# Gated attention and MLP mix on one core: five buffers of exponentials instead of six, a reordered start of attention, late products every second cycle, and one weight load behind shifted copies

## The chip, the cores and the metric

The kernel runs on one core of one Trainium2 chip. The core has five engines that work side by side and wait for each other through semaphores: TensorE (PE in the profile; its weight loads are PEld), VectorE (DVE), ScalarE (ACT), GpSimd (POOL) and SyncE (SP), which here issues most of the transfers. The metric is device time in microseconds (us). The kernel before takes 921.9 us as the median of 3 runs (921.63 to 922.75).

## The reference

The input x has 2048 tokens of 448 features. Two branches work on it, and a gate per token mixes them (cut to what matters):

```python
x = A_x                                             # (1, 2048, 448)
g = sigmoid((x * gate_w).sum(-1, keepdims=True))
# A: attention, 16 heads of 28 features, one key and one value head for all
q = (x @ wq) in 16 heads;  k = x @ wk;  v = x @ wv
p = softmax(q k^T * 28 ** -0.5);  a = concat(p v) @ wo
# B: shifts along the tokens, then an MLP
h  = gelu(layernorm(x) @ w1)
hs = concat(four quarters of h, shifted by +1, -1, +2, -2 tokens) @ w2
x1 = x + hs
b  = x1 + gelu(layernorm(x1) @ w3) @ w4
out = g * a + (1 - g) * b
```

## The kernel before

Everything is in one program without loops on the chip; the Python loops unroll. Each engine runs its instructions in the order in which the Python code issues them (`manual_schedule` over all five engines), and a semaphore wait is put ahead of an instruction whose data or whose buffer is not yet free. So the order in the code sets the order of work on every queue, SP's included.

Matrices are split into a high and a low part (`wh`, `wl`, `ah`, `al`), and a product is three matrix products that accumulate in one bank of PSUM.

**Stage 1** (to about 126 us) makes the queries, keys and values, the product with w1 (`stage_w1`) and the product with w2 (`stage_w2`). For the shifts, `spare_h(b)` copies rows of `hl` into the spare partitions of `hh` and `hl` with four transfers (L433 to L436); the last block's products with w2 read those spare partitions. At the end of stage 1 three things are issued on SP, in this order: `load_w34(0, s2a)`, which loads the first 256 columns of w3 (L611) and the first 256 rows of w4 (L612) into `w34raw`; `xt_read(0, ...)`, which loads the normalised x1 of the first block in transposed form into `xr` (L177 and twice L179); and `spare_h(NB - 1)`.

**Stage 2** (126 to about 401 us) is the MLP with w3 and w4, four blocks of 512 tokens. A piece of it is left for later: the products of the last 128 rows of w4 for the last block (`w4_late`, `gf_late`) are cut into 8 jobs, two halves of the columns for each of 4 tiles of tokens. A job is 16 matrix products (L843) and one add into `x1` by DVE (L878). That add needs rows of `x1` which POOL has multiplied with 1 - g (`weigh_x1`, L670).

**Stage 3** (about 401 to 908 us) is attention. A unit u is one block of 512 queries and a group of 4 heads; there are 16 units, and each goes over 16 key tiles of 128 keys. The loop runs over cycles c of two key tiles each, 128 in all; c = 8u + i. PSUM has 8 banks: four singles (`bank_0` to `bank_3`) and two pairs (`pair_0`, `pair_1`). In a cycle TensorE does, in this order:

- the scores of the first tile (L205, for 4 heads): heads 0 and 1 into two singles, heads 2 and 3 into `pairs[0]`;
- the scores of the second tile: into the other two singles and `pairs[1]`;
- the values of the two tiles of the cycle before (L892): exponentials `p` times `vext`, one half of the queries into the first single of this cycle (`s0`), the other half into the second (`s1`), each once ScalarE has read the scores there;
- one job, if there is one (L843), into the free half of `s0`.

ScalarE makes the exponentials (L258) in this order: first tile, heads 0 and 1, one by one; second tile, heads 0 and 1, one by one; second tile, heads 2 and 3 at once from `pairs[1]`; first tile, heads 2 and 3 at once. These last two heads DVE has copied from `pairs[0]` into the tile `p` before (L939), so that the pair is free early, and ScalarE works there in place. DVE also adds the values to the output (L813, L817). The exponentials of a key tile are one tile `p`; its pool has `PB = 6` buffers, used in turn. The first key tile's `p_0_0` is in another pool.

In cycle 0 the first tile's scores are already there: they were made in stage 2, between the products with w4, in the four singles. So cycle 0 makes the scores of the second tile, in `bank_2`, `bank_3` and `pair_1`, and then two w4 jobs, in `bank_0` and `bank_1`. Cycles 1 to 6 do one w4 job each; cycles 7 to 11 have no job. From cycle 12 on (unit 1, i = 4) there are jobs of the product with wo, 8 for each unit, and each cycle does one.

Of the kernel before, what the change touches and what calls it, by code (L numbers as in the profile page):

```python
# [29 lines left out]
SCALE = DH ** -0.5  # L30
EPS = 1e-5
SHIFTS = (-1, 1, -2, 2)
PB = 6
MK = 16
LIMIT = 1e18

# [1 line left out]
def f32(ap):  # L38
    return ap.bitcast(F32)
# [3 lines left out]
def gated_mix_kernel(  # L43
# [12 lines left out]
    nc = tc.nc  # L56
# [14 lines left out]
    first = keep.tile([P, 4], F32, name="first")  # L71
# [103 lines left out]
    def xt_read(b, raw):  # L175
        xd = xd_of.pop(b)
        nc.sync.dma_start(raw[:, 0:3, :], xd[0:12].rearrange("(c f) i p u -> (f i) c (p u)", c=3))  # L177
        for k in (0, 64):
            nc.sync.dma_start(raw[k:k + 64, 3, :], xd[12:14].rearrange("f i p u -> (f i) (p u)"))  # L179
# [16 lines left out]
    def q_low(u):  # L196
        nc.vector.tensor_sub(ql_of[u], qr_of.pop(u), f32(qh_of[u]))

    def scores(u, kt, ps):
        kh = kh_of[0]  # L200
        keys = slice(kt * P, (kt + 1) * P)
        for r, (k, q) in enumerate(((kh, qh_of[u]), (kh, ql_of[u]), (kl, qh_of[u]))):
            for j in range(4):
                h = slice(32 * j, 32 * j + 32)
                nc.tensor.matmul(ps[j], k[h, keys], q[h, :], start=(r == 0), stop=(r == 2), tile_position=(32 * j, 0))  # L205
# [51 lines left out]
    def exps(p, heads, source=None):  # L257
        nc.scalar.activation(p[:, heads], p[:, heads] if source is None else source, AF.Exp, scale=SCALE)  # L258
# [4 lines left out]
    with tc.tile_pool(name="s1b", bufs=1) as s1b, \  # L263
            tc.tile_pool(name="ps1", bufs=1, space=PSUM) as ps1:
        s1_stack = ExitStack()
        s1 = s1_stack.enter_context(tc.tile_pool(name="s1", bufs=1))
# [154 lines left out]
        def shifted(t, m, k):  # L421

            c = [1 + SHIFTS[i] - SHIFTS[0] + 516 * i for i in range(m, m + k)]
            flat = f32(t)[C:P].rearrange("i m n -> i (m n)")
            if k == 1:
                return flat[:, c[0]:c[0] + 512]
            step = c[1] - c[0]
            o = min(c[0], 4 * 516 - 2 * step)
            return flat[:, o:o + 2 * step].rearrange("i (m n) -> i m n", m=2)[:, :, c[0] - o:c[0] - o + 512]

        def spare_h(b):
            low = f32(hl[b])
            nc.sync.dma_start(shifted(hh[b], 0, 2), low[0:32, 0, 1:513])  # L433
            nc.sync.dma_start(shifted(hh[b], 2, 2), low[32:64, 0, 1:513])
            nc.sync.dma_start(shifted(hl[b], 1, 2), low[64:96, 0, 1:513])
            nc.sync.dma_start(shifted(hl[b], 3, 1), low[96:112, 0, 1:513])  # L436
# [158 lines left out]
        s2a = ctx2.enter_context(tc.tile_pool(name="s2a", bufs=1, side="right", reuse_waits="tile"))  # L595
# [4 lines left out]
        def big(name):  # L600
            return bigs.tile([P, 2048], F32, tag="big", bufs=2, name=name)

        def load_w34(i, pool):
            w3h.append(pool.tile([P, 4, 2 * P], F32R, name=f"w3h_{i}"))
            w3l.append(pool.tile([P, 4, 2 * P], F32R, name=f"w3l_{i}"))
            w4h.append(pool.tile([P, 2, D], F32R, name=f"w4h_{i}"))
            w4l.append(pool.tile([P, 2, D], F32R, name=f"w4l_{i}"))
            raw = big(f"w34raw_{i}")
            raw3[i] = raw[:, 0:1024].rearrange("p (c n) -> p c n", c=4)
            raw4[i] = raw[:, 1024:1024 + 2 * D].rearrange("p (c n) -> p c n", c=2)  # L610
            nc.sync.dma_start(raw3[i], w3[:, :, i * 256:i * 256 + 256])  # L611
            nc.sync.dma_start(raw4[i], w4[i * 256:i * 256 + 256, :].rearrange("(c p) n -> p c n", p=P))  # L612
# [27 lines left out]
                    nc.vector.tensor_sub(hi[64:128], raw[64:128], f32(hi)[64:128])  # L640

        xraw2[0] = big("xr_0").rearrange("p (c n) -> p c n", c=4)
        load_w34(0, s2a)
        xt_read(0, xraw2[0])
        spare_h(NB - 1)

        def third(t):
            if t == 0:
# [17 lines left out]
    with tc.tile_pool(name="s2", bufs=1, reuse_waits="tile") as s2, \  # L666
# [35 lines left out]
        for b in range(NB):  # L702
            acc = [ps2.tile([P, 512], F32, tag="acc", bufs=4, name=f"acc_{b}_{t}") for t in range(4)]
            gs = {}
            for f in range(NF):
# [26 lines left out]
                if b == 1 and f == 1:  # L732
                    nc.gpsimd.memset(khd, 0.0)
                    for j in range(4):
                        h = slice(32 * j, 32 * j + DH)
# [33 lines left out]
    with tc.tile_pool(name="s3", bufs=1, reuse_waits="tile") as s3, \  # L769
# [4 lines left out]
        pairs = [ps3.tile([P, 2, 512], F32, name=f"pair_{i}") for i in range(2)]  # L774
# [105 lines left out]

        p_of = {0: p_first}

        def score_tiles(u, kt, first, second, pair):
            scores(u, kt, [first, second, pair[:, 0], pair[:, 1]])
            p_of[u * NT + kt] = p = s3.tile([P, 4, 512], F32, tag="p", bufs=PB, name=f"p_{u}_{kt}")
            return p

# [7 lines left out]
                    p_of.pop(k)  # L895

        jobs = [(w4_products, w4_add, (t,), cols) for t in range(4) for cols in halves]
        left, right, both = slice(0, 1), slice(1, 2), slice(2, 4)
        sums, norms, later = [], [], []
        pv = None  # L900
        MAX_AT = 2
# [1 line left out]
        def job_products(ps, n):  # L903
            adds = []
            for _ in range(min(n, len(jobs))):
                products, add, args, cols = jobs.pop(0)
                part = ps[:, 0:D // 2] if n == 1 else ps[:, cols]
                products(*args, part, cols)
                adds.append((add, args, part, cols))
            return adds  # L910
# [5 lines left out]
        def run_jobs(ps, n):  # L916
            job_adds(job_products(ps, n))

        NC = NU * NT // 2
        HINTS = {8 * NT // 2 + 4: [mybir.EngineType.SP],  # L920
                 14 * NT // 2 - 2: [mybir.EngineType.DVE, mybir.EngineType.Activation]}
        for c in range(NC):
            u, i = divmod(c, NT // 2)
            k = 2 * c
            s0, s1, s2, s3_ = singles if c % 2 == 0 else singles[2:] + singles[:2]
            if c:
                pa = score_tiles(u, 2 * i, s0, s1, pairs[0])
                with tc.block() if c in HINTS else nullcontext():
                    if c in HINTS:
                        tc.mark_branch_hint_location("redo", "LikelyTaken", HINTS[c])  # L930
                    exps(pa, left, s0.unsqueeze(1))
                exps(pa, right, s1.unsqueeze(1))
            if i == 2 and u == 0:
                q_begin(1)
            if i == 3 and u == 0:
                q_low(1)
                q_fetch(2)
            if 0 < c < NC - 1:
                nc.vector.tensor_copy(pa[:, both], pairs[0])  # L939
            elif c:  # L940
                exps(pa, both, pairs[0])
            if i == 3 and later:
                later.pop(0)()
            if i == 1 and sums:
                norms.append(recip(*sums.pop()))
            if i == (3 if u == NU - 1 else 4) and norms:
                w = norms[0][0]
                norm(*norms.pop())
            if i == 5 and u + 2 < NU:
                q_begin(u + 2)  # L950
            if i == 6 and u + 2 < NU:
                q_low(u + 2)
                q_fetch(u + 3)
            pb = score_tiles(u, 2 * i + 1, s2, s3_, pairs[1])
            exps(pb, left, s2.unsqueeze(1))
            exps(pb, right, s3_.unsqueeze(1))
            exps(pb, both, pairs[1])
            if 0 < c < NC - 1:
                exps(pa, both)
            if u and i == (3 if u == NU - 1 else 4):  # L960
                jobs += [(wo_products, wo_add, (u - 1, t), cols) for t in range(4) for cols in halves]
            if c == 0:
                run_jobs(s0, 1)
                run_jobs(s1, 1)
                continue
            v = (c - 1) // (NT // 2)
            at_max = i == MAX_AT and u + 1 < NU
            q0, q1 = slice(0, 256), slice(256, 512)
            values((k - 2, k - 1), s0[:, q0], q0)
            values_end(v, s0[:, q0], q0)  # L970
            if at_max:
                max_part(u + 1, range(4), pairs[0][:, 0])
                later.append(lambda u=u: max_end(u + 1))
            elif i == MAX_AT:
                run_jobs(pairs[0][:, 0], 1)
            values((k - 2, k - 1), s1[:, q0], q1)
            adds = job_products(s0[:, q1], 1)
            values_end(v, s1[:, q0], q1)
            job_adds(adds)
            if i == 0 and v < NU - 1:  # L980
                sums.append(sums_begin(v))
        assert not sums and not norms and not later and len(jobs) == 3

        u = NU - 1
# [7 lines left out]

        for k in (2 * NC - 2, 2 * NC - 1):
            for i in range(2):
# [60 lines left out]
        with tc.If(again > 0, label="redo"):  # L1055
            for b in range(NB):
                for g in range(NG):
                    u = b * NG + g
# [6 lines left out]
                    for kt in range(NT):  # L1065
                        ps = [bank(f"s2_{u}_{kt}_{j}") for j in range(4)]
                        scores(u, kt, ps)
                        p = s3.tile([P, 4, 512], F32, tag="p", bufs=PB, name=f"p2_{u}_{kt}")
                        for j in range(4):
# [7 lines left out]
                    for t in range(4):  # L1077
                        ps = bank(f"wo2_{u}_{t}")[:, whole]
# [55 lines left out]
```

## Time and profile before

| what | time |
|---|---|
| median of 3 runs | 921.9 us |
| lowest and highest of them | 921.63 and 922.75 us |
| the profiled execution | 921.32 us |
| its span, from the first to the last instruction | 919.5 us |
| granted clock of TensorE | 1.00 in all of it |

1.8 us of the profiled execution lie outside the span. Times in the rows that follow are from the start of the span. A row of the timeline gives the start, the length, the engine, the line, the operation, output and inputs, the shapes, how many instructions the row merges, and in brackets the idle time ahead of it with what ended it. Buffer numbers are left out of the names there: `bank` is any of the four singles, `pair` any of the two pairs, `p` any tile of exponentials. The ends of matrix products are modelled, and they overlap in the array, so that a row's length is more than the time from one product to the next.

### The profile page before, as it was taken

Reading aid. Unit: us, or ns where it says so; the run is one execution under the profiler, and the core shown is the slowest. Engines: PE = TensorE matmul, PEld = TensorE weight load, DVE = VectorE, ACT = ScalarE, POOL = GpSimd, SP = SyncE. Lnnn points to the kernel's source line nnn. Section 1 sums busy time; section 2 is a strip of 40 time slices with the busy share of each in tenths; the row PEclk is TensorE's granted clock in tenths of the full one; section 3 lists DMA queues with packets and bytes.
Section 4 is the critical chain, followed back from the end, with each engine's and each line's share of the span. In section 5 each row is a group of like instructions: output and inputs, shape, how many; then the busy total and the mean of one; then the engine's idle time right before and its main releaser. Section 6 shows DMA issues by size and latency. Waiting matters only on the chain.

```text
span 919.5 us, 24276 instructions
## 1 busy us (share of the span) xinstructions
PE 907.3 (99%) x10360; PEld 626.2 (68%) x10360; DVE 516.7 (56%) x961; ACT 636.9 (69%) x1003; POOL 78.6 (9%) x116
## 2 busy tenths in 40 slices
PE   9999999999999999999999999999999999999998
PEld 6788888888888888865555555555555555555554
DVE  3674274631441431146676776777667767767665
ACT  5442255322222222269999999999999999999995
POOL 3153420200000520020000000000000000000000
PEclk9999999999999999999999999999999999999999
DMA  9832643120110110010000001000011000010001
GB/s 300 274 102 66 174 134 127 40 66 1 41 47 1 40 46 1 1 52 24 17 23 23 15 22 48 24 25 15 25 33 37 24 18 20 15 54 14 15 14 43
DMA packets 40583, 47.32 MB, mean 51 GB/s; under 512 B 10136, under 2 KB 28632, under 8 KB 40472
## 3 DMA queue, kind: packets, MB, share of 16 engines
q1 hardware_dynamic: 37304, 40.30, 15.2%
q10 hardware_dynamic: 3168, 5.44, 1.6%
q8 instruction: 82, 1.34, 0.6%
q14 instruction: 29, 0.24, 0.1%
HBM read 32.56 MB, written 11.67 MB: 48 GB/s over the span
## 4 chain that ended last, share of the span: by engine, by line
PE 92%; ACT 4%; DMA 1%; issue 1%; DVE 0%; SPq 0%; POOL 0%; ACTq 0%
PE bank L892 26%; PE bank L205 17%; PE bank L843 5%; PE acc L700 5%; PE acc L698 5%; PE acc L699 5%; PE g L136 4%; PE g L137 4%; PE g L138 4%; ACT p L258 4%; PE pair L205 1%; PE g L139 1%; PE g L140 1%; PE h L137 1%; PE h L136 1%; PE h L138 1%
## 5 line engine op out<-in xcount | busy, mean ns | idle before, releaser
L258 ACT ACTIVATE p<-bank 128x512 f32<-128x512 f32 x514 | 267.0, 610 | 9.0 <-PE bank L205 2.0
L892 PE MATMUL bank<-p,vext 128*32 128x256 f32 x4064 | 247.7, 382 | 5.5 <-ACT p L258 1.0
L892 PEld LDWEIGHTS bank<-p,vext 128*32 128x32 f32 x4064 | 117.6, 109 | 123.2 <-ACT p L258 60.0
L939 DVE COPY p<-pair 128x1024 f32<-128x1024 f32 x126 | 154.3, 1225 | 57.2 <-PE pair L205 43.3
L688 ACT ACTIVATE gh<-g 128x512 fp32r<-128x512 f32 x55 | 33.0, 599 | 182.6 <-PE g L140 182.6
L817 DVE TENSOR_TENSOR o<-o,bank 128x256 f32<-128x256 f32 x222 | 93.5, 421 | 86.0 <-PE bank L892 72.2
L258 ACT ACTIVATE p<-p 128x1024 f32<-128x1024 f32 x126 | 138.8, 1102 | 0.0
L258 ACT ACTIVATE p<-pair 128x1024 f32<-128x1024 f32 x129 | 137.4, 1065 | 0.0
L690 DVE TENSOR_TENSOR gl<-gf,gh 128x512 fp32r<-128x512 f32 x55 | 38.3, 697 | 166.4 <-ACT gf L689 166.4
L205 PE MATMUL bank<-qh,kh 32*128 32x512 f32 x514 | 115.5, 443 | 0.3 <-DVE x L878 0.2
L205 PE MATMUL pair<-qh,kh 32*128 32x512 f32 x510 | 114.3, 443 | 0.0
L205 PE MATMUL bank<-qh,kl 32*128 32x512 f32 x514 | 102.1, 389 | 0.0
L205 PE MATMUL bank<-ql,kh 32*128 32x512 f32 x514 | 102.0, 389 | 0.0
L205 PE MATMUL pair<-qh,kl 32*128 32x512 f32 x510 | 101.1, 389 | 0.0
L205 PE MATMUL pair<-ql,kh 32*128 32x512 f32 x510 | 100.8, 389 | 0.0
L205 PEld LDWEIGHTS bank<-qh,kh 32*128 32x128 f32 x514 | 48.1, 181 | 62.8 <-issue 38.0
L700 PE MATMUL acc<-w4h,gl 128*128 128x448 f32 x220 | 80.7, 367 | 0.0
L698 PE MATMUL acc<-w4h,gh 128*128 128x448 f32 x220 | 80.1, 364 | 0.0
L699 PE MATMUL acc<-w4l,gh 128*128 128x448 f32 x220 | 79.8, 363 | 0.0
L843 PE MATMUL bank<-wof,on 128*32 128x224 f32 (+1 forms) x984 | 69.5, 357 | 0.1
L137 PE MATMUL g<-al,w3h 128*128 128x512 f32 x168 | 65.4, 389 | 0.0
L136 PE MATMUL g<-ah,w3h 128*128 128x512 f32 x168 | 65.4, 389 | 0.0
(206 smaller groups left out, 1393.0 us busy)
## 6 DMA issues: line engine op xcount, KB each, us to landing
qd<-qf ACTq DMA_DIRECT2D x15, 256.0 KB
rb<-rd SPq DMA_DIRECT2D x15, 256.0 KB
x<-in_x_dram SPq DMA_DIRECT2D x4, 896.0 KB
xd<-xt SPq DMA_DIRECT2D x16, 224.0 KB
w34raw<-in_w_dram SPq DMA_DIRECT2D x7, 512.0 KB
qr<-qd SPq DMA_DIRECT2D x64, 56.0 KB
w34raw<-in_w_dram SPq DMA_DIRECT2D x7, 448.0 KB
out_dram<-ot SPq DMA_DIRECT2D x14, 224.0 KB
```

The source lines that it names most:

```text
L136: nc.tensor.matmul(ps, wh[:, c, :], ah[:, c, :], start=(c == 0), stop=False)
L137: nc.tensor.matmul(ps, wh[:, c, :], al[:, c, :], start=False, stop=False)
L138: nc.tensor.matmul(ps, wl[:, c, :], ah[:, c, :], start=False, stop=False)
L205: nc.tensor.matmul(ps[j], k[h, keys], q[h, :], start=(r == 0), stop=(r == 2), tile_position=(32 * j, 0))
L258: nc.scalar.activation(p[:, heads], p[:, heads] if source is None else source, AF.Exp, scale=SCALE)
L698: nc.tensor.matmul(ps, gh[:, tok], w4h[i][:, k, :], start=(f == 0), stop=False)
L699: nc.tensor.matmul(ps, gh[:, tok], w4l[i][:, k, :], start=False, stop=False)
L700: nc.tensor.matmul(ps, gl[:, tok], w4h[i][:, k, :], start=False, stop=(f == stop))
L817: nc.vector.tensor_add(o, o, pv)
L843: nc.tensor.matmul(ps[32 * i:32 * i + 32, :], a[:, c:c + 32], w, start=start, stop=stop, tile_position=(0, 32 * i))
L892: nc.tensor.matmul(pv[32 * j:32 * j + 32, :], vext[:, kt, :], p_of[k][:, j, qs], start=(k == ks[0]), stop=(k == ks[-1]), tile_position=(0, ...
L939: nc.vector.tensor_copy(pa[:, both], pairs[0])
```

## The change

Four edits, in the words of the code:

- `PB` goes from 6 to 5.
- `load_w34(0, s2a)` moves behind `spare_h(NB - 1)`, so that on SP the two loads of w3 and w4 come behind the transfers of `xr` and the four copies of `spare_h`.
- In cycle 0 the second tile's scores go into the four singles alone, and the third tile's scores, which were cycle 1's first ones, follow at once, in the two pairs. DVE copies heads 0 and 1 of the third tile out of `pair_0`, and ScalarE takes heads 2 and 3 from `pair_1` and then the copy. Cycle 0 now does three w4 jobs, two in `bank_2` and one in `bank_3`. The two pairs then change their parts for the rest (`pairs.reverse()`), and cycle 1 has only its second tile left.
- The other five w4 jobs are in cycles 3, 5, 7, 9 and 11, one each, instead of cycles 1 to 6.

```diff
-PB = 6
+PB = 5
...
         xraw2[0] = big("xr_0").rearrange("p (c n) -> p c n", c=4)
-        load_w34(0, s2a)
         xt_read(0, xraw2[0])
         spare_h(NB - 1)
+        load_w34(0, s2a)
...
-        def score_tiles(u, kt, first, second, pair):
-            scores(u, kt, [first, second, pair[:, 0], pair[:, 1]])
+        def score_tiles(u, kt, first, second, third, fourth):
+            scores(u, kt, [first, second, third, fourth])
             p_of[u * NT + kt] = p = s3.tile([P, 4, 512], F32, tag="p", bufs=PB, name=f"p_{u}_{kt}")
             return p
...
-        left, right, both = slice(0, 1), slice(1, 2), slice(2, 4)
+        left, right, both, front = slice(0, 1), slice(1, 2), slice(2, 4), slice(0, 2)
...
         NC = NU * NT // 2
+        JOBS_0 = (2, 1)
+        IDLE = range(2, 12, 2)
...
         for c in range(NC):
             u, i = divmod(c, NT // 2)
             k = 2 * c
             s0, s1, s2, s3_ = singles if c % 2 == 0 else singles[2:] + singles[:2]
-            if c:
-                pa = score_tiles(u, 2 * i, s0, s1, pairs[0])
+            if c == 0:
+                pb = score_tiles(u, 1, s2, s3_, s0, s1)
+                for j, ps in enumerate((s2, s3_, s0, s1)):
+                    exps(pb, slice(j, j + 1), ps.unsqueeze(1))
+                pa = score_tiles(u, 2, *(q[:, h] for q in pairs for h in range(2)))
+                nc.vector.tensor_copy(pa[:, front], pairs[0])
+                for ps, n in zip((s2, s3_), JOBS_0):
+                    run_jobs(ps, n)
+                exps(pa, both, pairs[1])
+                exps(pa, front)
+                pairs.reverse()
+                continue
+            if c > 1:
+                pa = score_tiles(u, 2 * i, s0, s1, pairs[0][:, 0], pairs[0][:, 1])
...
-            if 0 < c < NC - 1:
+            if 1 < c < NC - 1:
                 nc.vector.tensor_copy(pa[:, both], pairs[0])
-            elif c:
+            elif c > 1:
                 exps(pa, both, pairs[0])
...
-            pb = score_tiles(u, 2 * i + 1, s2, s3_, pairs[1])
+            pb = score_tiles(u, 2 * i + 1, s2, s3_, pairs[1][:, 0], pairs[1][:, 1])
             exps(pb, left, s2.unsqueeze(1))
             exps(pb, right, s3_.unsqueeze(1))
             exps(pb, both, pairs[1])
-            if 0 < c < NC - 1:
+            if 1 < c < NC - 1:
                 exps(pa, both)
...
-            if c == 0:
-                run_jobs(s0, 1)
-                run_jobs(s1, 1)
-                continue
...
-            adds = job_products(s0[:, q1], 1)
+            adds = job_products(s0[:, q1], 0 if c in IDLE or c == 1 else 1)
```

What this does to the order on the engines is shown at three places. In these rows a bracket names the semaphores that an instruction waits for.

The first place is ScalarE in two cycles of unit 5, as they stand in every cycle of attention but the first few: the tiles 8 to 11, where `p_5_8` and `p_5_10` are first tiles of their cycles. Before:

```order
L258 ACTIVATE p_5_8_6007<-bank_0_3209 128x512 [waits PE_49,Activation_49]
L258 ACTIVATE p_5_8_6007<-bank_1_3210 128x512 [waits PE_49]
L258 ACTIVATE p_5_9_6025<-bank_2_3211 128x512 [waits DVE_49,PE_49]
L258 ACTIVATE p_5_9_6025<-bank_3_3212 128x512 [waits PE_49]
L258 ACTIVATE p_5_9_6025<-pair_1_3259 128x1024 [waits PE_49]
L258 ACTIVATE p_5_8_6007<-p_5_8_6007 128x1024 [waits DVE_49]
L258 ACTIVATE p_5_10_6066<-bank_2_3211 128x512 [waits PE_49,Activation_49]
```

And in the changed kernel:

```order
L258 ACTIVATE p_5_8_6007<-bank_0_3209 128x512 [waits PE_49]
L258 ACTIVATE p_5_8_6007<-bank_1_3210 128x512 [waits PE_49]
L258 ACTIVATE p_5_9_6025<-bank_2_3211 128x512 [waits DVE_49,PE_49,Activation_49]
L258 ACTIVATE p_5_9_6025<-bank_3_3212 128x512 [waits PE_49]
L258 ACTIVATE p_5_9_6025<-pair_0_3258 128x1024 [waits PE_49]
L258 ACTIVATE p_5_8_6007<-p_5_8_6007 128x1024 [waits DVE_49]
L258 ACTIVATE p_5_10_6066<-bank_2_3211 128x512 [waits PE_49]
```

The instructions and their order are the same. With six buffers a cycle's first tile always gets a buffer that an earlier first tile had, whose last write was ScalarE's own, in place, and so the first exponentials of a cycle wait for ScalarE's semaphore beside TensorE's. With five buffers, first and second tiles change buffers in turn, and that second wait moves to the first exponentials of the second tile.

The second place is SP at the end of stage 1. Before:

```order
L611 DMA w34raw_1064<-in_w_dram 128x4x256 [waits DMAHW5_49,PE_49]
L612 DMA w34raw_1064<-in_w_dram 128x2x448 [waits DMAHW6_49]
L177 DMA xr_1059<-xd_892 128x3x512 [waits DMAHW7_49]
L179 DMA xr_1059<-xd_892 64x512 [waits DMAHW0_49]
L179 DMA xr_1059<-xd_892 64x512 [waits DMAHW1_49]
L433 DMA hh_957<-hl_958 16x2x512 [waits DMAHW2_49,Pool_49]
L434 DMA hh_957<-hl_958 16x2x512 [waits DMAHW3_49]
L435 DMA hl_958<-hl_958 16x2x512 [waits DMAHW4_49]
L436 DMA hl_958<-hl_958 16x512 [waits DMAHW5_49]
```

And in the changed kernel:

```order
L177 DMA xr_1059<-xd_892 128x3x512 [waits DMAHW5_49,PE_49]
L179 DMA xr_1059<-xd_892 64x512 [waits DMAHW6_49]
L179 DMA xr_1059<-xd_892 64x512 [waits DMAHW7_49]
L433 DMA hh_957<-hl_958 16x2x512 [waits DMAHW0_49,Pool_49]
L434 DMA hh_957<-hl_958 16x2x512 [waits DMAHW1_49]
L435 DMA hl_958<-hl_958 16x2x512 [waits DMAHW2_49]
L436 DMA hl_958<-hl_958 16x512 [waits DMAHW3_49]
L611 DMA w34raw_1071<-in_w_dram 128x4x256 [waits DMAHW4_49]
L612 DMA w34raw_1071<-in_w_dram 128x2x448 [waits DMAHW5_49]
```

The two weight loads go to the end. The wait for TensorE (a buffer of stage 1 that becomes free) stays with whichever transfer is first. The semaphores named DMAHW are eight that transfers use in turn, so that the load of w4 now waits for the first transfer of `xr`, which has the same one (5).

The third place is TensorE at the start of attention, from the last scores of the second key tile to the first values. Before:

```order
L205 MATMUL pair_1_3259<-qh0_1049,kl_77 128x512 x2
L843 MATMUL bank_0_3209<-w4_late_1052,gf_late_1051 32x224 x4
L843 MATMUL bank_1_3210<-w4_late_1052,gf_late_1051 32x224 x4
L205 MATMUL bank_2_3211<-qh0_1049,kh_1048 128x512 [waits Activation_49]
L205 MATMUL bank_3_3212<-qh0_1049,kh_1048 128x512 [waits Activation_49]
L205 MATMUL pair_0_3258<-qh0_1049,kh_1048 128x512 [waits DVE_49]
...
L205 MATMUL bank_0_3209<-qh0_1049,kh_1048 128x512 [waits DVE_49]
L205 MATMUL bank_1_3210<-qh0_1049,kh_1048 128x512 [waits DVE_49]
L205 MATMUL pair_1_3259<-qh0_1049,kh_1048 128x512 [waits Activation_49]
...
L892 MATMUL bank_2_3211<-p_0_0_3226,vext_78 32x256 [waits Activation_49]
```

And in the changed kernel:

```order
L205 MATMUL bank_1_3210<-qh0_1049,kl_77 128x512
L205 MATMUL pair_0_3258<-qh0_1049,kh_1048 128x512 [waits DVE_49]
...
L843 MATMUL bank_2_3211<-w4_late_1052,gf_late_1051 32x224 [waits Activation_49]
L843 MATMUL bank_2_3211<-w4_late_1052,gf_late_1051 32x224 x7
L843 MATMUL bank_3_3212<-w4_late_1052,gf_late_1051 32x224 [waits Activation_49]
L843 MATMUL bank_3_3212<-w4_late_1052,gf_late_1051 32x224 x3
L205 MATMUL bank_0_3209<-qh0_1049,kh_1048 128x512 [waits Activation_49]
L205 MATMUL bank_1_3210<-qh0_1049,kh_1048 128x512 [waits Activation_49]
L205 MATMUL pair_0_3258<-qh0_1049,kh_1048 128x512 [waits DVE_49]
...
L892 MATMUL bank_2_3211<-p_0_0_3226,vext_78 32x256 [waits DVE_49]
```

The third tile's scores stand ahead of the jobs, in the pairs. The fourth tile's scores wait for exponentials and for DVE's copy, no longer for the adds of the jobs (L878); that wait moves to the first values.

## The prediction

> **What bounds the kernel now.** I read the page first: the busy times and the chain of work that ended last.
>
> ```profile
> PE 907.3 (99%) x10360; PEld 626.2 (68%) x10360; DVE 516.7 (56%) x961; ACT 636.9 (69%) x1003; POOL 78.6 (9%) x116
> PE 92%; ACT 4%; DMA 1%; issue 1%; DVE 0%; SPq 0%; POOL 0%; ACTq 0%
> ```
>
> TensorE looks full, but 4% of the chain is ScalarE's, so somewhere TensorE waits for ScalarE, again and again. The chain by time and the timeline, in one cycle of attention (c = 20, and the start of 21), show where:
>
> ```profile
> 479.30 0.61 ACT p L258
> 479.91 0.04 issue
> 479.95 1.93 PE bank L892 x32
> ```
>
> ```profile
> 478.82 0.39 PE L205 MATMUL pair<-qh,kl 32*128 32x512 f32 x2
> 479.30 2.07 ACT L258 ACTIVATE p<-bank 128x512 f32<-128x512 f32 x4
> 479.50 0.39 PE L205 MATMUL bank<-qh,kl 32*128 32x512 f32 x2
> 479.52 0.39 PE L205 MATMUL pair<-qh,kl 32*128 32x512 f32 x2
> 479.95 1.93 PE L892 MATMUL bank<-p,vext 128*32 128x256 f32 x32
> 481.23 1.06 ACT L258 ACTIVATE p<-pair 128x1024 f32<-128x1024 f32 x1
> 481.70 0.56 PE L843 MATMUL bank<-wof,on 128*32 128x224 f32 x8
> 482.13 1.10 ACT L258 ACTIVATE p<-p 128x1024 f32<-128x1024 f32 x1
> 482.77 0.40 PE L205 MATMUL pair<-qh,kl 32*128 32x512 f32 x2
> 483.26 1.09 ACT L258 ACTIVATE p<-bank 128x512 f32<-128x512 f32 x2
> ```
>
> This is a closed loop over two engines: scores of the first tile end (478.82 + 0.39 = 479.21), ScalarE's first exponentials (0.61 from 479.30), values into the bank that they read (479.95), the job (481.70), the next scores (ready at 483.17), exponentials again at 483.26. The period is 3.96 here. A gap in this loop is paid once per cycle. One gap is between the scores' end and ScalarE's start: 0.09, at both places.
>
> **Part 1: five buffers.** The order shows that with six the loop's exponentials wait for TensorE and for ScalarE itself, with five for TensorE alone. The same instruction with one wait stands in cycles 2 and 3, where buffers are used for the first time; a long idle time ahead of it is there too, so I put beside it cycle 19, where ScalarE was idle as well and which has both waits.
>
> ```profile
> 408.13 0.39 PE L205 MATMUL pair<-qh,kl 32*128 32x512 f32 x2
> 408.55 2.07 ACT L258 ACTIVATE p<-bank 128x512 f32<-128x512 f32 x4 [0.41 <-PE pair L205]
> 412.27 0.39 PE L205 MATMUL pair<-qh,kl 32*128 32x512 f32 x2
> 412.69 2.07 ACT L258 ACTIVATE p<-bank 128x512 f32<-128x512 f32 x4 [0.21 <-PE pair L205]
> ...
> 474.11 1.10 ACT L258 ACTIVATE p<-p 128x1024 f32<-128x1024 f32 x1
> 474.87 0.39 PE L205 MATMUL pair<-qh,kl 32*128 32x512 f32 x1
> 475.35 1.09 ACT L258 ACTIVATE p<-bank 128x512 f32<-128x512 f32 x2
> ```
>
> One wait: 408.52 to 408.55 and 412.66 to 412.69, 0.03. Two waits: 475.26 to 475.35, 0.09, although ScalarE had been idle since 475.21. So the second wait costs about 0.06, not ScalarE's own pace. The Trainium skill ("Perfetto Trace Analysis", Identifying Dependency Chains) says that an instruction that waits on several engines may get an extra semaphore instruction put ahead of it; it has no price for one, and the trace's 0.09 against 0.03 agrees with it.
>
> Does the loop keep the 0.06? TensorE must be able to start the values earlier. Its last scores start at 479.52, the values at 479.95, 0.43 later; in cycle 2 the same two starts were, by the timeline, 0.36 apart, and without a wait for ScalarE the step is smaller still. I take it that 0.06 fits. ScalarE must also be able to go at the shorter period; cycles without a job show its own pace:
>
> ```profile
> 432.28 2.11 ACT L258 ACTIVATE p<-bank 128x512 f32<-128x512 f32 x4
> 436.05 2.16 ACT L258 ACTIVATE p<-bank 128x512 f32<-128x512 f32 x4
> ```
>
> That is 3.77, below 3.95 - 0.06 = 3.89. The wait that moves goes to the second tile's first exponentials. Their scores end at 479.50 + 0.39 = 479.89; ScalarE takes them in the middle of its four, about 479.30 + 2 x 0.49 = 480.28 (0.49 is (2.07 - 0.61) / 3). The margin of 0.39 holds one more wait of 0.06, and behind it stand only ScalarE's own later exponentials. The buffer itself is free: with five, that tile overwrites the first tile of two cycles before, whose values are the products that ran one cycle ago, over when the job followed at about 477.9, 2.3 before 480.28.
>
> The gain runs over the cycles with a job, from 13 to 127:
>
> ```profile
> 451.54 2.07 ACT L258 ACTIVATE p<-bank 128x512 f32<-128x512 f32 x4
> 904.38 1.09 ACT L258 ACTIVATE p<-bank 128x512 f32<-128x512 f32 x2
> ```
>
> 452.84 for 114 periods, 3.97 each. 114 x 0.06 = 6.8 by the rounded rows; the gap over the cycles lies between 0.08 and 0.10, so I take 0.055: **6.3**. Bounds: 0 (something else holds the period) and 114 x 0.07 = 8.0.
>
> **Part 2: weight loads behind the shifted copies.**
>
> ```profile
> 105.78 0.61 SPq L611 DMA_DIRECT2D w34raw<-in_w_dram  x1
> ...
> 115.51 0.36 PE L477 MATMUL hs<-w2x,hl 128*128 128x448 f32 x1
> 116.75 0.45 PE L474 MATMUL hs<-w2h,hh 128*128 128x448 f32 x1 [0.88 <-DMA hh<-hl]
> 117.04 0.83 ACT L111 CAST w3h<-w34raw 128x768 fp32r<-128x768 f32 x1
> 120.54 1.09 DVE L118 TENSOR_TENSOR w3l<-w34raw,w3h 128x256 fp32r<-128x256 f32 x3
> 125.92 0.39 PE L136 MATMUL g<-ah,w3h 128*128 128x512 f32 x1
> ```
>
> ```profile
> 108.86 7.75 DMA hh<-hl
> ```
>
> ```profile
> 105.80:125.90 20.10, 19.22 (x95) 17.34 (x94) 12.68 (x21) 7.67 (x14) 11.59 (x17) 1.00 0.59 167
> 125.90:397.00 271.10, 271.10 (x1281) 237.17 (x1280) 92.93 (x166) 81.36 (x147) 26.59 (x29) 1.00 0.15 42
> ```
>
> TensorE (first column behind the length) has nothing else to do from 115.87 to 116.75: it waits for a copy issued at 108.86 that took 7.75, behind 960 KB of weights. Issues on SP take about 0.6, so the copies go out some 1.3 earlier, and on the queue only `xr` stands ahead of them. If they land by 115.87 (1.3 earlier gives 115.3 even at the same 7.75) the 0.88 is gone. The two weight loads go out at about 110.05 and later; with 7.75 again they land near 118. ScalarE casts w3 at 117.04 now; 1 us later is hidden, because the first product with w3 comes at 125.92, behind the rest of w2, and DVE's parts of w3 at 120.54 need only the cast. Point where it turns: a landing after about 119, when DVE's queue, which also empties `hs`, would hold TensorE. Stage 2 has 271.10 busy of 271.10, so the gain carries on to the end: **0.88**, bounds 0 and 0.88 + 0.1.
>
> **Part 3: the start of attention and the spread jobs.**
>
> ```profile
> 398.96 2.44 DVE L764 TENSOR_TENSOR x<-x,acc 128x448 f32<-128x448 f32 x4 [7.24 <-PE acc L700]
> 401.71 1.09 ACT L258 ACTIVATE p<-bank 128x512 f32<-128x512 f32 x2 [1.50 <-POOL pick L865]
> 402.09 5.55 POOL L670 TENSOR_SCALAR x<-x,gi 128x448 f32<-128x448 f32 x4
> 404.04 0.85 PE L205 MATMUL bank<-qh,kh 32*128 32x512 f32 x2 [0.22 <-DVE x L878]
> ```
>
> Before, cycle 1's second scores wait for the adds of the two jobs (404.04), which wait for POOL. Cycle 2's exponentials begin at 408.55. After: the third tile's scores need the pairs, free after DVE's adds at 401.40, and end at about 402.25. Three jobs (0.5 each), the first once ScalarE has read its bank (401.71 + 0.61), fill 402.35 to 403.85; the fourth tile's scores 403.85 to 404.65; values from 404.7 for 1.87; the fifth tile's scores from 406.6, ready at 407.6. The third job's add needs POOL's second tile (402.09 + 2 x 1.39 = 404.87) and is done at 405.4, ahead of the second half of the values (405.6). ScalarE alone: 401.71 + 1.93 + 0.90 + 0.93 + 0.97 + 0.91 = 407.35. So cycle 2 begins at about 407.65, **0.90** earlier; if POOL's add holds the values, half of it, and without any gain 0.
>
> From there to cycle 13 it was 451.54 - 408.55 = 42.99. After: six cycles with a job (3, 5, 7, 9, 11, 12) at 3.89 and five without at 3.77, 42.19: **0.80** (0.5 if jobs still cost 3.95). Jobs at 5 of the former idle cycles end later, up to cycle 11; what reads these rows of `x1` is the mix after unit 1's jobs, which begin at cycle 12, so nothing is late by it. The tail stays.
>
> **Sum:** 6.3 + 0.88 + 0.90 + 0.80 = 8.9. The profiled execution took 921.32, so 912.4; the median of the runs, 921.9, is 0.6 above it, so **913.0**.
>
> **The rivals.**
>
> *The loop keeps its period.* Something that the chain doesn't name would hold 3.95, say TensorE's second scores, so that the values can't start earlier. For it: TensorE is 99% busy. Against it: the values start 0.05 after ScalarE's first exponentials end, in both cycles shown, and TensorE has the room worked out above. Part 1 and 0.3 of part 3 fall away: 921.9 - 0.88 - 0.90 - 0.5 = 919.6. A half gain (0.03 a cycle) gives about 916.
>
> *Slower: the moved wait breaks ScalarE's overlap.* The second tile's first exponentials now have three waits. If the added one let ScalarE run empty there, an instruction would cost its full 0.61 in place of 0.49, and the same on the next, 0.24 together; ScalarE's pace becomes 3.77 + 0.24 = 4.01, the bound, 0.06 above 3.95: + 6.8, and - 1.8 of the start: 926.9. It decides once the loss is over 0.18. Against it: this instruction has two waits already, and four exponentials still take 2.07.
>
> *A buffer short.* The Trainium skill ("Perfetto Trace Analysis", Optimization Strategy) reads a gap that repeats on the engine that should be full as a possible sign of too few buffers; by that rule fewer buffers would make the gap longer. As a mechanism here: if the second tile had to wait for the values of the cycle it is in (over about 481.9), ScalarE would stand from 480.28 for 1.6 in each of 114 cycles, + 182, about 1104. The order and the 2.3 of margin speak against it; by that rule's reading the trace does not agree here, since the gap stays the same 0.09 wherever buffers are long free.
>
> **How the numbers follow.** My forecast, about 913: 0.70. Half the gain in the loop (916): 0.10. No gain in the loop (919.6): 0.10. The edits cancel or do nothing: 0.03. Slower by ScalarE: 0.06; by buffers: 0.01. A measurement of this kernel can tell about 0.2% (1.8 us) from no change, so faster 0.90, same 0.03, slower 0.07. The low end takes the loop at 8.0 in place of 6.3: 911.3. The high end takes in the half gain and a part of the case beyond it, 917.5.
>
> **What would show it.** Right: the first exponentials of a cycle start 0.03 behind the scores and the cycle takes 3.89; TensorE has no wait of 0.88 for `hh`; the time from the start of attention to cycle 2 is shorter by 0.9. Wrong: a gap still of 0.09, a period of 3.95 with the gap gone (another link), ScalarE's four exponentials longer than 2.07, or a wait of DVE or TensorE near 119 for w3.

## The result and the profile after

The changed kernel takes 912.75 us as the median of 5 runs (912.09 to 913.13), against 921.9 for the kernel before (921.63 to 922.75): a ratio of 0.9899, 95% interval 0.9885 to 0.9913. The forecast was 913.0.

First the page of the profiled execution: its first line and the rows of busy times and of the chain. Before, the first line was

```profile
span 919.5 us, 24276 instructions
```

and after:

```profile
span 911.2 us, 24150 instructions
PE 904.7 (99%) x10360; PEld 627.6 (69%) x10360; DVE 517.1 (57%) x961; ACT 633.1 (69%) x1003; POOL 78.3 (9%) x116
PE 98%; ACT 2%; DVE 0%; issue 0%
```

Each engine does as many counted instructions as before, yet 126 instructions have gone. They are of the kind that isn't counted as busy; of ScalarE's semaphore instructions the trace has 308 before and 185 after, about one fewer for each cycle of attention. In cycle 20 before, such an instruction, 0.02 long, starts at 479.24, ahead of the exponentials at 479.30; after, none stands between the scores and the exponentials of the same cycle. The transfer has left the chain (1% before).

The same cycle as in the prediction, c = 20, in the timeline after:

```profile
476.73 0.40 PE L205 MATMUL pair<-qh,kl 32*128 32x512 f32 x2
477.15 2.07 ACT L258 ACTIVATE p<-bank 128x512 f32<-128x512 f32 x4
477.44 0.39 PE L205 MATMUL pair<-qh,kl 32*128 32x512 f32 x2
477.80 1.93 PE L892 MATMUL bank<-p,vext 128*32 128x256 f32 x32
480.62 0.39 PE L205 MATMUL pair<-qh,kl 32*128 32x512 f32 x1
481.04 1.08 ACT L258 ACTIVATE p<-bank 128x512 f32<-128x512 f32 x2
```

The first tile's scores end at 477.13 and at 481.01, ScalarE begins at 477.15 and 481.04: gaps of 0.02 and 0.03 where there were 0.09, and a cycle of 3.89 where there were 3.96. The four exponentials still take 2.07. TensorE's last scores and its values are 0.36 apart now (0.43 before).

Where the time went shows when five marks of each trace are compared: TensorE's first product at L136, the first exponentials, the first exponentials of cycles 2, 13 and 127. The differences of their start times:

| stretch | before | after | gain | forecast |
|---|---|---|---|---|
| start to first L136 | 16.38 | 17.00 | -0.62 | 0 |
| to the first exponentials | 381.76 | 380.81 | 0.95 | 0.88 (part 2) |
| to cycle 2 | 10.41 | 9.45 | 0.96 | 0.90 |
| to cycle 13 | 42.99 | 42.56 | 0.43 | 0.80 |
| to cycle 127 | 452.85 | 446.15 | 6.70 | 6.3 |
| to the end of the span | 15.1 | 15.2 | -0.1 | 0 |

The ends of the long stretch, after:

```profile
449.81 1.57 ACT L258 ACTIVATE p<-bank 128x512 f32<-128x512 f32 x3
895.96 1.09 ACT L258 ACTIVATE p<-bank 128x512 f32<-128x512 f32 x2
```

The first stretch is no effect of the change: over the thirteen traces of this study it lies between 16.2 and 17.0 with the same loads ahead of it.

### The profile page after: what moved, and what is told of

Same layout as the page of the kernel before. It is cut to its first block, busy times and chain, and to the rows that moved or that the text cites. A ratio compares the mean times of both kernels' runs of the same rounds, so it can differ in the third digit from the quotient of the medians.

```text
span 911.2 us, 24150 instructions
## 1 busy us (share of the span) xinstructions
PE 904.7 (99%) x10360; PEld 627.6 (69%) x10360; DVE 517.1 (57%) x961; ACT 633.1 (69%) x1003; POOL 78.3 (9%) x116
## 3 DMA queue, kind: packets, MB, share of 16 engines
q1 hardware_dynamic: 37304, 40.30, 15.1%
## 4 chain that ended last, share of the span: by engine, by line
PE 98%; ACT 2%; DVE 0%; issue 0%
PE bank L892 26%; PE bank L205 19%; PE bank L843 6%; PE acc L700 5%; PE acc L698 5%; PE acc L699 5%; PE g L137 4%; PE g L138 4%; PE g L136 4%; PE pair L205 3%; ACT p L258 2%; PE hs L474 1%; PE hs L475 1%; PE g L139 1%; PE g L140 1%; PE h L137 1%
## 5 line engine op out<-in xcount | busy, mean ns | idle before, releaser
L136 PE MATMUL g<-ah,w3h 128*128 128x512 f32 x168 | 65.5, 390 | 0.0
```

Of the source, the lines that this page charges most:

```text
L136: nc.tensor.matmul(ps, wh[:, c, :], ah[:, c, :], start=(c == 0), stop=False)
```

## The experiments

Two questions are open after this. Is it the extra wait that makes the 0.06 in each cycle, or the number of buffers, or that a first tile takes a second tile's buffer over? And does each smaller edit bring its own term? The table of stretches is given for all runs behind the experiments.

**Six buffers again.**

```diff
-PB = 5
+PB = 6
```

> The changed kernel with six buffers in one ring again. Theory (the extra wait): the first exponentials of a cycle wait for TensorE and for ScalarE again, the gap behind the scores is 0.09 and the cycle 3.95 once more; 114 x 0.0587 = 6.7 more than the changed kernel, 919.4 us. Rival A (the number of buffers counts, fewer is better): the same 919.4. Rival B (the hand-over of a buffer from second to first tile counts): the same 919.4. If the gain came from elsewhere: 912.8.

919.65 us (ratio to the kernel before 0.9983, 0.9974 to 0.9993). The span has 24272 instructions (24276 before), the gap is 0.09, the stretch from cycle 13 to 127 takes 452.90. So the first part of the change carries 6.9 of the 9.15 by the medians, and 6.75 by that stretch (452.90 against 446.15). This alone doesn't tell the three readings apart.

**Five buffers, split three and two.**

```diff
-p = s3.tile([P, 4, 512], F32, tag="p", bufs=PB, name=...)
+p = s3.tile([P, 4, 512], F32, tag="pb" if kt % 2 else "pa", bufs=2 if kt % 2 else 3, name=...)
```

> The changed kernel, five buffers still, but three of them for first tiles and two for second tiles alone. The order shows both waits (TensorE and ScalarE) on the first exponentials of a cycle. Theory (the extra wait): gap 0.09, cycle 3.95, 919.4 us. Rival A (the number of buffers): as with five, 912.8. Rival B (the hand-over): a first tile gets a first tile's buffer again, 919.4.

919.28 us (0.9976, 0.9967 to 0.9986). Its timeline at the same place:

```profile
477.17 0.39 PE L205 MATMUL pair<-qh,kl 32*128 32x512 f32 x1
477.63 2.07 ACT L258 ACTIVATE p<-bank 128x512 f32<-128x512 f32 x4
...
481.10 0.40 PE L205 MATMUL pair<-qh,kl 32*128 32x512 f32 x2
481.58 1.58 ACT L258 ACTIVATE p<-bank 128x512 f32<-128x512 f32 x3
```

477.56 to 477.63 and 481.50 to 481.58: 0.07 and 0.08 here. The mean over cycles 13 to 127 is 0.092; this mean, here and below, counts from the last product into a single, which ends a little ahead of the last one into the pair that these rows show. Five buffers, and no gain: the number (rival A) is out.

**Six buffers, with first and second tiles taking over each other's.**

```diff
-p = s3.tile([P, 4, 512], F32, tag="p", bufs=PB, name=...)
+p = s3.tile([P, 4, 512], F32, tag="px" if (kt + kt // 2) % 2 else "py", bufs=3, name=...)
```

> The changed kernel with two rings of three buffers; first and second tile change rings every cycle, so that a first tile takes over a second tile's buffer, as with five in one ring. The order shows both waits on the first exponentials of a cycle nevertheless. Theory (the extra wait): gap 0.09, cycle 3.95, 919.4 us. Rival A (the number): 919.4. Rival B (the hand-over): 912.8.

919.67 us (0.9983, 0.9973 to 0.9993), gap 0.092. A first tile takes over a second tile's buffer and there is no gain: the hand-over (rival B), and with it the reason that the part on the change gave in its words, is out too. Why the wait is there nevertheless can be seen in the order of ScalarE. With five in one ring, the second tile of cycle c - 1 takes the buffer of the first tile of c - 3 and waits for that tile's last exponentials, which come behind those of the second tile of c - 3. The first tile of cycle c takes just that second tile's buffer, and what it would wait for has been waited for already. With two rings of three, the second tile of c - 1 waits only for something of cycle c - 4, and the first tile of c needs a wait of its own. What counts is whether an earlier wait covers it.

**Seven buffers in one ring.**

```diff
-PB = 5
+PB = 7
```

> The changed kernel with seven buffers in one ring. The order shows TensorE's wait alone on the first exponentials of a cycle, as with five. Theory (the extra wait): gap 0.03, cycle 3.89, 912.8 us. Rival A (the number): no better than six, 919.4 or more. Rival B (the hand-over): 912.8.

912.66 us (0.991, 0.9893 to 0.9926), 24150 instructions as with five, 3.89 per cycle:

```profile
476.01 0.40 PE L205 MATMUL pair<-qh,kl 32*128 32x512 f32 x2
476.43 2.06 ACT L258 ACTIVATE p<-bank 128x512 f32<-128x512 f32 x4
...
479.91 0.38 PE L205 MATMUL pair<-qh,kl 32*128 32x512 f32 x1
480.32 2.07 ACT L258 ACTIVATE p<-bank 128x512 f32<-128x512 f32 x4
```

Two more buffers, the same time: seven does what five does because it, too, leaves the loop's exponentials with one wait.

**Four buffers.**

```diff
-PB = 5
+PB = 4
```

> The changed kernel with four buffers in one ring; both waits on the first exponentials of a cycle by the order. Theory (the extra wait): 919.4 us, since the buffers are still free in time: a second tile overwrites the second tile of two cycles before, whose values are over 2 us before. Rival A (fewer buffers, shorter): 912.8 or less.

919.93 us (0.9974, 0.9963 to 0.9985), gap 0.092, as with six. Together: both waits at 4, 5 (3 + 2), 6 and 6 (two rings), 919.3 to 919.9; one wait at 5 and 7, 912.7 and 912.75. The extra wait is shown to be the cause.

**Three buffers.**

```diff
-PB = 5
+PB = 3
```

> The changed kernel with three buffers. A second tile now overwrites the first tile of the cycle before, which the values of its own cycle read. TensorE's wait alone on the first exponentials of a cycle, as with five. Theory: the second tile's first exponentials wait for the values' end; per cycle 1.6 us more than 3.95, so about 1.65 x 126 = 208 more than the changed kernel, some 1120 us, and the gap behind the first tile's scores stays near 0.03. A reader for whom only the wait's parity counts: 912.8.

1065.6 us in one run. This is the prediction's "a buffer short", made true. In the timeline, one cycle:

```profile
504.89 1.10 ACT L258 ACTIVATE p<-bank 128x512 f32<-128x512 f32 x2
505.55 1.93 PE L892 MATMUL bank<-p,vext 128*32 128x256 f32 x32 [0.46 <-ACT p L258]
507.17 1.09 ACT L258 ACTIVATE p<-bank 128x512 f32<-128x512 f32 x2 [1.18 <-issue]
```

ScalarE makes the first tile's two exponentials, stands for 1.18, and starts the second tile's at 507.17. The gap behind the first tile's scores stays 0.03. The mechanism is as forecast, the price was too high: I had ScalarE wait for the end of the values (507.48), but it needs only the products that read the first of their two tiles, and goes on 0.31 earlier; from cycle 13 to 127 it is 584.31 - 446.15 = 138.2, 1.21 per cycle, not 1.65.

**Five buffers and nothing else.**

```diff
-PB = 6
+PB = 5
```

(in the kernel before)

> The kernel before with five buffers and nothing else. Theory: the gap of 0.03 from cycle 5 on, 118 or so cycles with a job at 3.89, none of the rest: 921.9 - 6.9 = 915.0. If the gain needs the other edits too: 919 to 922.

914.9 us (0.9923, 0.9901 to 0.9946). The stretch from cycle 13 to 127 takes 446.27, and the stretches ahead of cycle 2 are those of the kernel before. The gain doesn't need the other edits.

**The late jobs in a row.**

```diff
-        IDLE = range(2, 12, 2)
+        IDLE = range(7, 12)
```

> The changed kernel with its five late w4 jobs in cycles 2 to 6 instead of 3, 5, 7, 9 and 11. By the count of cycles with and without a job, from cycle 2 to 13, nothing changes: 912.8. Theory: five cycles without a job in a row end with longer instructions of ScalarE and a longer cycle 12, as in the kernel before (4.12 there): 0.2 more, 913.0. Rival: spreading carried the shorter start, then 913.6.

912.94 us (0.9895, 0.9878 to 0.9912), not to be told from 912.75. In the trace the stretch from cycle 2 to 13 takes 42.87 and not 42.56: behind the reordered start, spreading the jobs brings 0.3, a little more than the 0.2 expected. Cycle 12 takes 4.10 here, for the reason that I gave, and cycle 2, with a job, 4.30, which I had not forecast. What cycle 2 holds is read from rows further down: its values start late, by 0.24 here, it has further products of 0.12, and two waits stand at its end, for 0.06. With these, 3.89 becomes 4.31. The kernel before with five buffers alone, whose jobs are in a row too, has no late values there and takes 42.65, only 0.09 more than the changed kernel. So most of the 0.43 in the first table came with the wait (42.99 to 42.65), and what spreading mends is in the main the price of the new start. Two traces with the same order of work differ by up to 0.17 in this stretch (42.99 and 42.82 in the table below), so 0.09 is no more than a hint.

**The weight loads alone.**

```diff
-        load_w34(0, s2a)
         xt_read(0, xraw2[0])
         spare_h(NB - 1)
+        load_w34(0, s2a)
```

(in the kernel before)

> The kernel before with only the two weight loads behind the shifted copies. Theory: TensorE's wait for hh of 0.88 is gone (1.15 with the slow first product behind it), DVE's add for hs comes late near 121 and takes some 0.27 back: 921.9 - 0.9 = 921.0. Rival (the copies were late for another reason): 921.9.

920.53 us (0.9986, 0.9977 to 0.9995). From the first L136 to the first exponentials it takes 380.88, 0.88 less than before.

**The start and the spread jobs alone:** the changed kernel with six buffers and the weight loads at their old place.

```diff
-PB = 5
+PB = 6
...
+        load_w34(0, s2a)
         xt_read(0, xraw2[0])
         spare_h(NB - 1)
-        load_w34(0, s2a)
```

> The kernel before with only the reordered start and the spread jobs, six buffers. Theory: cycle 2 begins 0.96 earlier, relative to the start of attention, and cycle 13 another 0.3: 921.9 - 1.3 = 920.6. Rival (the start is paid back in the cycles after it): 921.9.

920.61 us (0.9992, 0.9982 to 1.0001): the runs alone don't tell it from no change. The trace does: 9.45 from the first exponentials to cycle 2, and 42.93 from there to cycle 13. The 0.95 is there; the further 0.3 isn't, with two waits in the loop.

All stretches together, in us (the start to the first L136 left out):

| kernel | from the first L136 to the first exponentials | to cycle 2 | to cycle 13 | to cycle 127 | gap, mean from cycle 13 on |
|---|---|---|---|---|---|
| before | 381.76 | 10.41 | 42.99 | 452.85 | 0.091 |
| after | 380.81 | 9.45 | 42.56 | 446.15 | 0.030 |
| six buffers | 380.83 | 9.46 | 42.84 | 452.90 | 0.092 |
| five as 3 + 2 | 380.80 | 9.50 | 42.71 | 452.98 | 0.092 |
| six in two rings | 380.84 | 9.45 | 43.00 | 452.88 | 0.092 |
| seven | 380.88 | 9.45 | 42.52 | 446.02 | 0.032 |
| four | 380.80 | 9.45 | 42.88 | 452.72 | 0.092 |
| three | 381.28 | 9.51 | 56.55 | 584.31 | 0.027 |
| five alone | 381.69 | 10.39 | 42.65 | 446.27 | 0.031 |
| jobs in a row | 380.83 | 9.44 | 42.87 | 446.22 | 0.034 |
| loads alone | 380.88 | 10.39 | 42.82 | 453.09 | 0.092 |
| start alone | 381.76 | 9.45 | 42.93 | 452.71 | 0.091 |

Each column but the third has two values (and the kernel with three buffers), and each of them goes with one edit.

**Two splits of the keys later.** In the kernel after, one new wait stands on TensorE's weight load; the rows are of ScalarE (w3 is there), VectorE, GpSimd and TensorE near it:

```profile
116.42 0.84 ACT L111 CAST w3h<-w34raw 128x768 fp32r<-128x768 f32 x1 [2.45 <-DMA w34raw<-in_w_dram]
117.85 0.68 DVE L638 TENSOR_TENSOR al<-xr,ah 128x512 fp32r<-128x512 f32 x1
117.95 1.74 POOL L357 TENSOR_TENSOR kl<-kl,kh 128x512 fp32r<-128x512 f32 x1
118.56 1.68 DVE L640 TENSOR_TENSOR ah<-xr,ah 64x512 fp32r<-64x512 f32 x1
120.28 0.62 DVE L479 TENSOR_TENSOR x<-x,hs 128x448 f32<-128x448 f32 x1
120.95 0.19 PEld L474 LDWEIGHTS hs<-w2h,hh 128*128 128x128 f32 x1 [0.38 <-DVE x L479]
```

Before, the same L640 came when GpSimd's split was over:

```profile
117.08 1.62 POOL L357 TENSOR_TENSOR kl<-kl,kh 128x512 fp32r<-128x512 f32 x1
118.00 1.25 DVE L638 TENSOR_TENSOR al<-xr,ah 128x512 fp32r<-128x512 f32 x1
119.28 0.69 DVE L640 TENSOR_TENSOR ah<-xr,ah 64x512 fp32r<-64x512 f32 x1
```

The experiment issues two of the four splits later:

```diff
-        for b in range(NB):
+        for b in range(NB - 2):
             split_k(b)
...
         stage_w2(NB - 1, weights)
+        for b in range(NB - 2, NB):
+            split_k(b)
```

> The changed kernel with the last two of GpSimd's four splits of the keys (L356, L357) behind the last products with w2, so that none of them runs beside VectorE's splits of xr (L638, L640). Theory (GpSimd's work slows VectorE's beside it): L640 takes 0.69 and not 1.68, the add of hs (L479) is not late, TensorE's weight load loses its wait of 0.38, and from TensorE's first product with x to the first exponentials it is 380.5 rather than 380.8 us; the total 912.5, not to be told from 912.75 by the runs. Rival (the earlier transfer of xr or w3 made VectorE slow): L640 stays at 1.68 and the stretch at 380.8.

```profile
115.68 1.62 POOL L357 TENSOR_TENSOR kl<-kl,kh 128x512 fp32r<-128x512 f32 x1
116.69 1.16 DVE L638 TENSOR_TENSOR al<-xr,ah 128x512 fp32r<-128x512 f32 x1
117.88 0.98 DVE L640 TENSOR_TENSOR ah<-xr,ah 64x512 fp32r<-64x512 f32 x1
118.40 1.62 POOL L357 TENSOR_TENSOR kl<-kl,kh 128x512 fp32r<-128x512 f32 x1
```

912.32 us (0.9898, 0.9882 to 0.9915), as the changed kernel by the runs. My edit didn't do what I said: nothing held the later splits back, and they still ran beside VectorE's, only at other moments. L640 takes 0.98, not 0.69; L638, which overlaps the other split, 1.16. TensorE's wait is gone, and the stretch takes 380.63, between the 380.8 of the rival and the 380.5 of the theory. So in three kernels with three arrangements an operation of VectorE is slow where it starts while one of GpSimd is under way. Where VectorE starts first, it is GpSimd that takes longer: after, L638 begins at 117.85, 0.10 ahead of GpSimd's split, and takes its 0.68, while the split takes 1.74 instead of 1.30. No run keeps the two engines apart at this place in the changed kernel, so that GpSimd's work is the cause is argued from these overlaps. The Trainium skill ("SBUF — State Buffer", Who interferes with whom) says that a VectorE operation with two inputs in SBUF and a GpSimd operation that reads SBUF share a pair of ports, which one of them holds for a whole instruction while the other stands. The trace agrees within some 0.15: L640's own 0.69 counted back from its end, 120.24, begins at 119.55, and GpSimd's split ends at 119.69.

## Why the prediction was right, and where it was off

*What bounds the kernel.* Right: a closed loop over TensorE and ScalarE, in which each gap is paid once per cycle. With one wait fewer the loop runs 0.059 faster in each of 114 periods, and it does so in the two of six buffer arrangements from four up that leave one wait.

*Part 1, 6.3; measured 6.70.* Mechanism right, the size a little low: I took 0.055 where the rounded rows said 0.06 and the mean gap fell from 0.091 to 0.030. The kernel after shows it once more inside itself. By the order, the first exponentials of cycles 3 and 4 still wait for ScalarE there, and those behind do not:

```profile
414.65 0.39 PE L205 MATMUL pair<-qh,kl 32*128 32x512 f32 x1
415.13 2.07 ACT L258 ACTIVATE p<-bank 128x512 f32<-128x512 f32 x4
```

That is cycle 4: scores end at 415.04, a gap of 0.09. One reading in this part was wrong: I let the wait move to the second tile's exponentials at the price of one more 0.06 there. Nothing was added there; the four exponentials take 2.07 as before, and the trace has about one semaphore instruction fewer per cycle on the whole. The waits of an instruction and its semaphore instructions aren't counted one to one. At the second tile's first exponentials of cycle 20 each trace has one such instruction; before it waits for one semaphore, after for two. By the Trainium skill ("Perfetto Trace Analysis", Identifying Dependency Chains) such instructions may be inserted where an instruction waits on several engines; the drop from 308 to 185 agrees with it for the first tile, and the second tile's third wait shows no further one.

*Part 2, 0.88; measured 0.95 after, 0.88 in the kernel with this edit alone.* The size is right by two errors that cancel. At the place itself the gain was larger. These are TensorE's products behind the wait before, and at the same place after (the product that starts at 115.51 before starts at 116.05 after, since this execution began later):

```profile
117.04 0.37 PE L475 MATMUL hs<-w2l,hh 112*128 112x448 f32 x1
```

```profile
116.05 0.36 PE L477 MATMUL hs<-w2x,hl 128*128 128x448 f32 x1
116.25 0.37 PE L474 MATMUL hs<-w2h,hh 128*128 128x448 f32 x1
116.46 0.36 PE L475 MATMUL hs<-w2l,hh 112*128 112x448 f32 x1
```

From that product to the second one behind the wait it is 117.04 - 115.51 = 1.53 before and 116.46 - 116.05 = 0.41 after: 1.12. The idle time of 0.88 was counted from the modelled end of a product, 0.16 later than the next could have started, and the first product behind a wait takes 0.09 longer. Then about 0.2 of it went to the add of hs, which came late behind L640 (1.12 - 0.95 = 0.17 after, 1.12 - 0.88 = 0.24 with this edit alone; with the two splits later, 380.81 - 380.63 = 0.18 comes back). I had put the turning point at a landing of w3 after about 119; w3 was there in time (ScalarE casts it at 116.42, where I had it land near 118), and the delay came from VectorE's own work, which started earlier and met GpSimd's.

*Part 3, start, 0.90; measured 0.96.* Right. Cycle 2 began 0.06 after the end of ScalarE's previous exponentials (406.11 + 1.09 in the rows below), near both limits that I had worked out.

*Part 3, cycle 2 to 13, 0.80; measured 0.43.* This is the term that was off. I gave every cycle with a job 3.89 and every one without 3.77. Three things were missed. Cycle 2 takes 3.91, not 3.77. Its second tile's scores wait for ScalarE to read a pair, and it holds 16 products that I had overlooked (L212, `max_part` for the next unit):

```profile
406.11 1.09 ACT L258 ACTIVATE p<-pair 128x1024 f32<-128x1024 f32 x1
407.25 0.50 PE L205 MATMUL pair<-qh,kh 32*128 32x512 f32 x2
407.26 2.06 ACT L258 ACTIVATE p<-bank 128x512 f32<-128x512 f32 x4
...
408.14 1.07 PE L892 MATMUL bank<-p,vext 128*32 128x256 f32 x16
409.03 0.30 PE L212 MATMUL pair<-khd,qh 128*32 128x64 bf16 x16
409.14 1.05 PE L892 MATMUL bank<-p,vext 128*32 128x256 f32 x16
...
410.12 0.49 PE L205 MATMUL bank<-qh,kh 32*128 32x512 f32 x2
...
411.17 1.08 ACT L258 ACTIVATE p<-bank 128x512 f32<-128x512 f32 x2
```

The values start 0.88 behind the first exponentials, where it is 0.65 in cycle 4, and from there to the next scores it takes 1.98, where it is 1.86 in cycle 4. The second wait at the cycle's end adds 0.06: together 0.23 + 0.12 + 0.06 = 0.41 more than in cycle 4. There TensorE has 0.26 of room, since ScalarE takes up the next scores 1.26 after they began, and 1.00 after it in a cycle with a job (cycle 5). 0.41 - 0.26 = 0.15. By these numbers none of the three alone would have made the cycle longer. Cycle 3 has two waits at its end as well and takes 3.96. And a cycle with a job behind one without takes 3.92 (cycle 9, from 434.30): when ScalarE comes to its exponentials without a pause, the four take 2.10 and not 2.06, and the first of them, which the values wait for, 0.63 and not 0.60:

```profile
434.30 2.10 ACT L258 ACTIVATE p<-bank 128x512 f32<-128x512 f32 x4
438.22 2.06 ACT L258 ACTIVATE p<-bank 128x512 f32<-128x512 f32 x4
442.00 2.11 ACT L258 ACTIVATE p<-bank 128x512 f32<-128x512 f32 x4
```

0.14 + 0.07 + 4 x 0.03 = 0.33 of the missing 0.37. That the 0.63 is the cause of the 3.92 is borne out by the run with the jobs in a row: there five cycles without a job follow each other, the first exponentials of cycles 8 to 12 take 0.63, 0.68, 0.73, 0.78 and 0.82, the values start 0.05 behind each of them, and cycle 12, the first with a job again, takes 4.10, 0.21 above 3.89, with first exponentials 0.22 above 0.60.

*The rivals.* "The loop keeps its period" fell: TensorE had the 0.06, and the step from its last scores to the values shrank from 0.43 to 0.36. "ScalarE's overlap breaks" fell: 2.07. "A buffer short" fell with five buffers and came true with three.

## What to carry to other kernels

In a closed loop over two engines, count the waits of the instruction at each hand-over: one more semaphore instruction cost 0.06 us here, and 6.7 us over 114 cycles. The number of buffers in a ring decides not only whether a buffer is free in time but also whether an earlier wait already covers the new one; so list the waits for neighbouring ring sizes, and try the smaller one too. Split a gain by stretches between the same instructions of both traces: terms of 0.3 to 1 us that the runs can't tell apart stand out there.

## What was not expected of the hardware

Moving a wait to an instruction that already had two cost nothing that the trace shows, while taking one from an instruction with two saved 0.06 each time. And VectorE's subtraction of 64 x 512 took 0.69 alone, 0.98 and 1.68 beside GpSimd's, whose subtraction itself went from 1.30 to 1.62 and 1.74: an earlier transfer made it earlier, and so slower.
